# Long convolution with a gate: the last phase's first tiles kept in the filter spectrum's dead tile and loaded from six pairs ahead

## The chip, the core and the metric

The kernel runs on one core of a Trainium2 chip. A core has five engines with instruction streams of their own: TensorE (PE; its weight loads are shown as PEld), VectorE (DVE), ScalarE (ACT), GpSimd (POOL) and SyncE (SP), which only issues transfers. Transfers are moved by 16 DMA engines; here they are issued from SP, ACT and POOL. The metric is the device time of one execution in microseconds (us), as the median of several runs.

## The reference

Two layers, one after the other. The first is a long convolution: `u = x * v` for 4 batches of 12800 positions and 128 channels is convolved along the positions with a filter that a small network makes from a position table, and the result is multiplied by `x`. The second is a gated projection with a convolution of five taps.

```python
h_filt = (np.maximum(pos_emb @ w1, 0.0) @ w2) * window
u = x * v
Uf = np.fft.rfft(u, n=2 * S, axis=1)
Hf = np.fft.rfft(h_filt, n=2 * S, axis=0)
y = np.fft.irfft(Uf * Hf[None], n=2 * S, axis=1)[:, :S]
z = x * y
gate = sigmoid(sum(conv_w[k] * shifted(z, K - 1 - k) for k in range(5)))
out = (gate * (z @ w_val)) @ w_out
```

## The kernel before

Everything is float32. The sequence of 12800 is seen as 2 halves (`J`) of 100 x 64 (`N1`, `N2`), and the convolution is done by transforms of these lengths, as matrix products. There are three phases.

*Phase 1* makes the product of x and v, transforms it along N1 and stores it in DRAM as `a_u`; beside it the filter is transformed into `ag`, a tile of 128 x 12800 floats (51,200 bytes on each partition), the filter's spectrum.

*Phase 2* runs over 50 pairs `p` of rows of the spectrum (`NP = 50`). For a pair, SP loads `a_u` four pairs ahead (L201) and now and then a table of weights (L194); TensorE transforms (L486) and makes the pair's filter from columns 256p to 256p + 255 of `ag` (L467); VectorE multiplies (L492); GpSimd adds (L568, L571); TensorE transforms back. The first half of the result goes through `c_sb` (ScalarE, L508) to the DRAM tile `c_y`, issued from ScalarE (L509). The second half goes through `c_raw` (ScalarE, L530), two pair-steps later GpSimd makes sum and difference of it in `c_both` (L537, two buffers), and it is stored in the DRAM tile `c_z` (L538), from ScalarE for pairs up to 47 and from GpSimd for 48 and 49. Pair 49's `c_y` is stored in two pieces, one copied by ScalarE and issued there, one copied by VectorE and issued from SP (L511 to L514).

*Phase 3* runs over 32 groups of four rows. Group `s` needs its rows of `c_y` or `c_z`: two tiles (`c` = 0, 1) of 100 rows x 2048, each loaded by `load_part(s, c, i)` in three pieces (`PARTS`): `i = 0` are 64 rows (pairs 0 to 31), `i = 1` are 32 (pairs 32 to 47), `i = 2` are 4 (pairs 48 and 49). It needs 0.8 MB of x too (`load_x`, tile `xr`). For each row TensorE multiplies with `inv` (`sd`, L661), ScalarE copies (L666), TensorE transposes (`tp`, L673), ScalarE copies a part (`dif`, L675), VectorE adds and subtracts (`yr`, two buffers, L683 and L684), and GpSimd multiplies with x (L686) into a tile `tail` (for the first group and the 17th) or `ext` (two buffers, each 4 rows of halo and 16 rows). Ten rows later come the taps on VectorE (L703), the sigmoid on ScalarE, the two projections on TensorE (L715, L725) and the output's store.

The order in each engine's stream is that in which the code emits (the loops of phases 2 and 3 are under `manual_schedule`). Rows of groups lie in six tiles `ld` of 128 x 2048, shared with `a_u` and the weights: `buffer()` gives the one that comes free first, and SP waits for its last reader. In phase 2 pieces of the groups 0 to 2 are loaded by the table `early`; the rest and the first three x tiles are loaded at the start of phase 3, when `ag` has been given back.

A transfer issued from SP or ACT counts one of eight completion counters (DMAHW0 to DMAHW7). The program gives them out in turn, in an order of transfers that is fixed when it is built, over both streams; a transfer is issued when the one that had its counter before has landed. Transfers from GpSimd have counters of their own (DMASW).

Of the kernel before, what the change touches and what calls it, by code (L numbers as in the profile page):

```python
# [117 lines left out]
def tile_longconv_gate(  # L118
# [321 lines left out]
    def load_part(s, c, i):  # L440
        j, g = y_order[s]
        if (s, c) not in rows_in:
            rows_in[s, c] = buffer(NP + 1 + s)
        k0, n, step, p0 = PARTS[i]
        to = rows_in[s, c][p0:p0 + step * (n - 1) + 1:step]
        m, n0 = divmod(g * R, H2)
        if j == 0:
            n0 += m * N2 + c * H2
            nc.sync.dma_start(out=to, in_=c_y[k0:k0 + n, n0:n0 + R].rearrange("k p e -> k (p e)"))
        else:  # L450
            if m:
                n0 = H2 - R - n0
            nc.sync.dma_start(
                out=to.rearrange("k (q f) -> k q f", q=2),
                in_=c_z[k0:k0 + n, m, :, c, n0:n0 + R].rearrange("k q i e -> k q (i e)"))

    with tc.tile_pool(name="p2", bufs=1, reuse_waits="tile") as p2, \
# [38 lines left out]
        def inverse(p, vt):  # L496
# [9 lines left out]
            to = c_y[2 * p:2 * p + 2].rearrange("h p e -> p h e")  # L506
            if p < NP - 1:
                nc.scalar.copy(out=c_sb, in_=c_ps)  # L508
                nc.scalar.dma_start(out=to, in_=c_sb)  # L509
            else:  # L510
                nc.scalar.copy(out=c_sb[:, 0], in_=c_ps[:, 0])  # L511
                nc.scalar.dma_start(out=to[:, 0], in_=c_sb[:, 0])
                nc.vector.tensor_copy(out=c_sb[:, 1], in_=c_ps[:, 1])
                nc.sync.dma_start(out=to[:, 1], in_=c_sb[:, 1])  # L514
# [18 lines left out]
        def butterfly(p):  # L533
            raw = raw_p.pop(p)
            both = p2.tile([128, 2, 2, HB], F32, name="c_both", bufs=2)
            for m, op in enumerate((ALU.add, ALU.subtract)):
                nc.gpsimd.tensor_tensor(both[:, :, m], raw[:, :, 1], raw[:, :, 0], op=op)  # L537
            (nc.scalar if p < NP - 2 else nc.gpsimd).dma_start(  # L538
                out=c_z[2 * p:2 * p + 2].rearrange("h s q c i e -> (q c i) (h s) e"),
                in_=both.rearrange("p h s e -> p (h s) e"))  # L540

        filt_p, z_p, v_p, raw_p = {}, {}, {}, {}
        AHEAD = 4

        early = {NP - 5: [(0, 0, 0)], NP - 4: [(0, 1, 0)], NP - 3: [(1, 0, 0)], NP - 2: [(1, 1, 0)],
                 NP - 1: [(0, 0, 1), (0, 1, 1), (2, 0, 0)]}
        with tc.manual_schedule():
            for p in range(-1, NP + 2):
# [43 lines left out]
                for s, c, i in early.get(p, ()):  # L592
                    load_part(s, c, i)

    ag_pool.__exit__(None, None, None)

    with tc.tile_pool(name="p3", bufs=1, reuse_waits="tile") as p3, \
# [7 lines left out]
        tails, exts, loads3, sds, tps, gate_sg, gate_gt, outs3 = {}, {}, {}, {}, {}, {}, {}, {}  # L611

        def load_x(s):
            j, g = y_order[s]
            xr = p3.tile([D, R * ROW], F32, name="xr", bufs=3)
            nc.sync.dma_start(out=xr, in_=xt[j][:, g * R:(g + 1) * R].rearrange("d n b a -> d (n b a)"))
            loads3[s] = xr
# [212 lines left out]


# [39 lines left out]
```

## Time and profile before

| | |
|---|---|
| median of three runs | 1068.72 us |
| lowest and highest run | 1066.05, 1074.51 us |
| the profiled execution, its own time | 1072.18 us |
| span of its instructions | 1070.4 us |
| busy in the span: PE, DVE, POOL, ACT | 973.9, 972.7, 747.4, 625.9 us |
| mean granted clock of TensorE | 0.977 |
| phase 1, to about 332 us: mean DMA rate | 349 GB/s |
| pair loop, 332 to 680 us: mean DMA rate | 316 GB/s |

The span runs from the first instruction to the last. Busy time is an average over stages with different limits: which engine bounds a stage is seen where it has no gaps. In the rows of the timeline the columns are start in us, length in us, engine (SPq and ACTq are the issues of transfers by SP and ScalarE), line, operation, output and input, their shapes, the count of instructions merged in the row, and in brackets the idle time of the engine before it and what ended that. A merged row stands at the start of its first instruction. In the row of a stretch of time the columns are its bounds, its length, the busy time and count of PE, PEld, DVE, ACT and POOL, the granted clock of TensorE, the busy share of the DMA engines and the rate in GB/s.

### The profile page before, as it was taken

Reading aid. Unit: us, or ns where it says so; the run is one execution under the profiler, and the core shown is the slowest. Engines: PE = TensorE matmul, PEld = TensorE weight load, DVE = VectorE, ACT = ScalarE, POOL = GpSimd, SP = SyncE. Lnnn points to the kernel's source line nnn. Section 1 sums busy time; section 2 is a strip of 40 time slices with the busy share of each in tenths; the row PEclk is TensorE's granted clock in tenths of the full one; section 3 lists DMA queues with packets and bytes.
Section 4 is the critical chain, followed back from the end, with each engine's and each line's share of the span. In section 5 each row is a group of like instructions: output and inputs, shape, how many; then the busy total and the mean of one; then the engine's idle time right before and its main releaser. Section 6 shows DMA issues by size and latency. Waiting matters only on the chain. (4 is left out here: it accounts for less than half of the span.)

```text
span 1070.4 us, 21514 instructions
## 1 busy us (share of the span) xinstructions
PE 973.9 (91%) x8080; PEld 510.3 (48%) x8080; DVE 972.7 (91%) x1061; ACT 625.9 (58%) x1017; POOL 747.4 (70%) x465
## 2 busy tenths in 40 slices
PE   2778799999968999999999999779999999999996
PEld 0344466556624555556545555334444444444442
DVE  8878999699938999989999999379999999999997
ACT  1545587798853444434444434367677777777774
POOL 2223222222225999999999999689999999999990
PEclk9989899999988999999999999899999999999999
DMA  8999899988987999979989997977788888888813
GB/s 279 374 345 388 325 381 370 394 327 329 397 290 268 335 317 334 341 277 339 345 307 334 344 335 266 335 294 267 276 294 309 269 295 305 275 300 286 294 75 123
DMA packets 97152, 330.16 MB, mean 308 GB/s; under 512 B 12691, under 2 KB 37883, under 8 KB 81051
## 3 DMA queue, kind: packets, MB, share of 16 engines
q1 hardware_dynamic: 41848, 196.90, 53.8%
q10 hardware_dynamic: 49522, 111.37, 26.9%
q0 software_dynamic: 5680, 20.53, 5.0%
q8 instruction: 66, 1.08, 0.4%
q14 instruction: 36, 0.29, 0.1%
HBM read 197.67 MB, written 131.07 MB: 307 GB/s over the span
## 5 line engine op out<-in xcount | busy, mean ns | idle before, releaser
L686 POOL TENSOR_TENSOR ext<-yr,xr 128x400 f32<-128x400 f32 x120 | 307.7, 2566 | 27.8 <-DVE yr L684 24.5
L703 DVE SCALAR_TENSOR_TENSOR gt<-ext,cw,gt 128x1600 f32<-128x1600 f32 (+1 forms) x132 | 255.1, 1932 | 0.1
L397 POOL DMA_DIRECT2D a_u<-st x64 | 34.4, 537 | 227.5 <-ACT st L389 223.7
L389 ACT COPY st<-fp 128x1024 f32<-128x1024 f32 x128 | 129.7, 1031 | 86.3 <-PE fp L388 42.4
L537 POOL TENSOR_TENSOR c_both<-c_raw 128x512 f32<-128x512 f32 x100 | 126.6, 1295 | 9.8 <-DMA c_z<-c_both 8.7
L530 ACT COPY c_raw<-c_ps 128x1024 f32<-128x1024 f32 x50 | 50.8, 1016 | 140.2 <-PE c_ps L525 124.6
L661 PE MATMUL sd<-ld,inv 128*64 128x512 f32 x512 | 126.5, 612 | 6.7 <-DMA ld<-c_y 6.4
L492 DVE TENSOR_TENSOR va<-z_ps,h_sb 128x2048 f32<-128x2048 f32 x50 | 114.1, 2283 | 20.2 <-PE z_ps L486 20.1
L568 POOL TENSOR_TENSOR va<-va,vb 128x1024 f32<-128x1024 f32 x49 | 116.9, 2386 | 20.2 <-DVE vb L492 17.9
L486 PE MATMUL z_ps<-ld,ld 64*64 64x512 f32 x800 | 112.2, 613 | 19.0 <-DMA ld<-a_u 8.2
L492 DVE TENSOR_TENSOR vb<-z_ps,h_sb 128x2048 f32<-128x2048 f32 x50 | 114.2, 2285 | 13.8 <-POOL va L571 13.8
L666 ACT COPY sd_sb<-sd 128x512 f32<-128x512 f32 x128 | 75.9, 593 | 73.7 <-PE sd L661 61.9
L725 PE MATMUL o_ps<-gd,wout 128*128 128x400 f32 x256 | 111.4, 517 | 8.3 <-DVE gd L720 6.8
L388 PE MATMUL fp<-ld,fsd 64*128 64x512 f32 x320 | 88.6, 656 | 30.7 <-ACT st L389 15.6
L715 PE MATMUL v_ps<-ext,wval 128*128 128x400 f32 x252 | 105.3, 500 | 0.0
L571 POOL TENSOR_TENSOR va<-va,vb 128x1024 f32<-128x1024 f32 x42 | 101.2, 2408 | 0.0
L502 PE MATMUL c_ps<-va,ld 64*64 64x512 f32 x800 | 97.3, 600 | 1.4 <-DVE va L568 1.4
L673 PEld LDWEIGHTS tp<-ident,sd_sb 128*128 128x128 f32 x512 | 58.4, 141 | 77.0 <-PE sd L661 49.6
L720 DVE TENSOR_TENSOR gd<-v_ps,sg 128x400 f32<-128x400 f32 x126 | 84.2, 669 | 0.2 <-ACT sg L708 0.2
L673 PE MATMUL tp<-ident,sd_sb 128*128 128x128 f32 x512 | 80.1, 280 | 3.8 <-DVE yr L684 2.7
L508 ACT COPY c_sb<-c_ps 128x1024 f32<-128x1024 f32 x49 | 49.7, 1014 | 55.5 <-PE c_ps L502 55.5
L683 DVE TENSOR_TENSOR yr<-tp,dif 128x204 f32<-128x204 f32 x128 | 58.8, 459 | 23.9 <-ACT dif L675 23.8
(108 smaller groups left out, 1814.5 us busy)
## 6 DMA issues: line engine op xcount, KB each, us to landing
ld<-a_u SPq DMA_DIRECT2D x48, 1024.0 KB
a_u<-st ACTq DMA_DIRECT2D x62, 512.0 KB
xr<-in_xt_dram SPq DMA_DIRECT2D x32, 800.0 KB
c_y<-c_sb ACTq DMA_DIRECT2D x49, 512.0 KB
out_dram<-o_sb ACTq DMA_DIRECT2D x31, 800.0 KB
c_z<-c_both ACTq DMA_DIRECT2D x48, 512.0 KB
ld<-in_xv_dram SPq DMA_DIRECT2D x40, 512.0 KB
a_u<-st POOLq DMA_DIRECT2D x64, 256.0 KB, 6.3
```

The lines of the kernel that those rows point to most:

```text
L389: nc.scalar.copy(out=st[:, c], in_=fp.rearrange("k j e -> k (j e)"))
L486: nc.tensor.matmul(out=z[half[h], c], lhsT=wk[half[c], 0, half[h]], rhs=a2[half[c], h, j], start=True, stop=True)
L492: nc.vector.tensor_tensor(out, z.rearrange("p (b d) -> p b d", d=D).unsqueeze(1).to_broadcast([128, n, B, D]), h_sb.unsqueeze(2).to_broadc ...
L537: nc.gpsimd.tensor_tensor(both[:, :, m], raw[:, :, 1], raw[:, :, 0], op=op)
L568: (nc.gpsimd if nxt else nc.vector).tensor_tensor(va[:, 0:2], va[:, 0:2], vb[:, 0:2], op=ALU.add)
L571: nc.gpsimd.tensor_tensor(va[:, 2:4], va[:, 2:4], vb[:, 2:4], op=ALU.add)
L661: nc.tensor.matmul(out=to, lhsT=inv[:, 2 if j * m * c else c], rhs=t, start=True, stop=True)
L673: nc.tensor.transpose(out=tp[:, b], in_=t[:, b], identity=ident)
L686: nc.gpsimd.tensor_tensor(e[:, r0 + r], yr, xr, op=ALU.mult)
L703: nc.vector.scalar_tensor_tensor(gt, rows(t, k)[:, cols], cw[:, k:k + 1], gt, op0=ALU.mult, op1=ALU.add)
L715: nc.tensor.matmul(out=v_ps, lhsT=wval, rhs=rows(t)[:, r * ROW:(r + 1) * ROW], start=True, stop=True)
L725: nc.tensor.matmul(out=o_ps, lhsT=wout, rhs=gd, start=True, stop=True)
```

## The change

The first three x tiles, the rows of the second group (`s == 1`) and one of the two `ext` buffers get fixed places in `ag`, whose columns of low number have been read by then: x at columns 0 to 4799 (1600 for each of three), the two row tiles at 4800 and 6848, and the `ext` buffer over the same columns from 4800 to 12799. `ag` lives to the end, and the `p3` pool holds neither `xr` nor that `ext`. The x tiles of all later groups use the three places in turn. The table `early` starts one pair sooner and holds more; pair 49's `c_y` is stored in one piece; the `c_z` stores are taken out of `butterfly` into `store`, and pair 46's is issued a pair later, together with pair 47's.

```diff
     ag = ag_pool.__enter__().tile([128, N1, J, FO], F32, name="ag")
+    AG = ag.rearrange("p k j e -> p (k j e)")
+    XW = R * B * N1
...
         if (s, c) not in rows_in:
-            rows_in[s, c] = buffer(NP + 1 + s)
+            at = 3 * XW + c * 2048
+            rows_in[s, c] = AG[:, at:at + 2048] if s == 1 else buffer(NP + 1 + s)
...
+    def load_x(s):
+        j, g = y_order[s]
+        xr = AG[:, s % 3 * XW:(s % 3 + 1) * XW]
+        nc.sync.dma_start(out=xr, in_=xt[j][:, g * R:(g + 1) * R].rearrange("d n b a -> d (n b a)"))
+        loads3[s] = xr
...
             c_sb = p2.tile([128, 2, BD], F32, name="c_sb", bufs=3)
-            to = c_y[2 * p:2 * p + 2].rearrange("h p e -> p h e")
-            if p < NP - 1:
-                nc.scalar.copy(out=c_sb, in_=c_ps)
-                nc.scalar.dma_start(out=to, in_=c_sb)
-            else:
-                nc.scalar.copy(out=c_sb[:, 0], in_=c_ps[:, 0])
-                nc.scalar.dma_start(out=to[:, 0], in_=c_sb[:, 0])
-                nc.vector.tensor_copy(out=c_sb[:, 1], in_=c_ps[:, 1])
-                nc.sync.dma_start(out=to[:, 1], in_=c_sb[:, 1])
+            nc.scalar.copy(out=c_sb, in_=c_ps)
+            nc.scalar.dma_start(out=c_y[2 * p:2 * p + 2].rearrange("h p e -> p h e"), in_=c_sb)
...
                 nc.gpsimd.tensor_tensor(both[:, :, m], raw[:, :, 1], raw[:, :, 0], op=op)
+            both_p[p] = both
+
+        def store(p):
             (nc.scalar if p < NP - 2 else nc.gpsimd).dma_start(
                 out=c_z[2 * p:2 * p + 2].rearrange("h s q c i e -> (q c i) (h s) e"),
-                in_=both.rearrange("p h s e -> p (h s) e"))
+                in_=both_p.pop(p).rearrange("p h s e -> p (h s) e"))
...
-        early = {NP - 5: [(0, 0, 0)], NP - 4: [(0, 1, 0)], NP - 3: [(1, 0, 0)], NP - 2: [(1, 1, 0)],
-                 NP - 1: [(0, 0, 1), (0, 1, 1), (2, 0, 0)]}
+        early = {NP - 6: ["x0"], NP - 5: [(1, 0, 0), "x1"], NP - 4: [(0, 0, 0), (1, 1, 0)], NP - 3: [(0, 1, 0)],
+                 NP - 2: [(2, 0, 0), (0, 0, 1), (0, 1, 1), (1, 0, 1), (1, 1, 1)]}
...
                 if 0 <= p - 2:
                     butterfly(p - 2)
-                for s, c, i in early.get(p, ()):
-                    load_part(s, c, i)
-
-    ag_pool.__exit__(None, None, None)
+                    for q in () if p == NP - 2 else (p - 3, p - 2) if p == NP - 1 else (p - 2,):
+                        store(q)
+                for what in early.get(p, ()):
+                    if what in ("x0", "x1"):
+                        load_x(int(what[1]))
+                    else:
+                        load_part(*what)
...
         def new_ext(j, q):
-            e = p3.tile([D, HALO + EG * R, B, N1], F32, name="ext", bufs=2)
-            exts[j, q] = e
+            if not ext_buf:
+                ext_buf.append(AG[:, 3 * XW:].rearrange("d (n b a) -> d n b a", b=B, a=N1))
+                ext_buf.append(p3.tile([D, HALO + EG * R, B, N1], F32, name="ext"))
+            exts[j, q] = ext_buf[len(exts) % 2]
...
         with tc.manual_schedule():
-            load_x(0)
-            for c, i in ((0, 2), (1, 2)):
-                load_part(0, c, i)
-            for c, i in ((0, 1), (1, 1), (0, 2), (1, 2)):
-                load_part(1, c, i)
-            load_x(1)
+            for s in range(2):
+                for c in range(2):
+                    load_part(s, c, 2)
             for c, i in ((0, 1), (0, 2), (1, 0), (1, 1), (1, 2)):
                 load_part(2, c, i)
             load_x(2)
...
+    ag_pool.__exit__(None, None, None)
```

ScalarE at the seam, before: from pair 48's `c_y` store to the first copy of phase 3. The names are those of the tiles, with the program's numbers; the three `c_z` sources in this part are pair 46 (`c_both_6161`), pair 47 (`c_both_6217`), and the `c_raw` tiles are pair 48's (`6215`) and pair 49's (`6249`). In brackets stand the counters that an instruction waits for.

```order
L509 DMA c_y_61<-c_sb_6158 128x2x512 [waits DMAHW1_49,Activation_49]
L538 DMA c_z_62<-c_both_6161 128x4x256 [waits DMAHW2_49,Pool_49]
L511 COPY c_sb_6185<-c_ps_6176 128x512 [waits DMAHW3_49,PE_49]
L512 DMA c_y_61<-c_sb_6185 128x512 [waits Activation_49]
L530 COPY c_raw_6215<-c_ps_6190 128x1024 [waits PE_49]
L538 DMA c_z_62<-c_both_6217 128x4x256 [waits DMAHW0_49,Pool_49]
L530 COPY c_raw_6249<-c_ps_6224 128x1024 [waits PE_49]
L666 COPY sd_sb_6295<-sd_6289 128x512 [waits PE_49]
```

The same place in the change (`c_both_6164` is pair 46, `c_both_6221` pair 47, `c_raw_6219` and `c_raw_6251` are pairs 48 and 49):

```order
L518 DMA c_y_61<-c_sb_6161 128x2x512 [waits DMAHW0_49,Activation_49]
L517 COPY c_sb_6191<-c_ps_6182 128x1024 [waits DMAHW7_49,PE_49]
L518 DMA c_y_61<-c_sb_6191 128x2x512 [waits DMAHW1_49,Activation_49]
L534 COPY c_raw_6219<-c_ps_6194 128x1024 [waits PE_49]
L545 DMA c_z_62<-c_both_6164 128x4x256 [waits DMAHW7_49,Pool_49]
L545 DMA c_z_62<-c_both_6221 128x4x256 [waits DMAHW0_49,Pool_49]
L534 COPY c_raw_6251<-c_ps_6226 128x1024 [waits PE_49]
L667 COPY sd_sb_6289<-sd_6283 128x512 [waits DVE_49,PE_49]
```

Both `c_z` stores now stand together behind pair 49's `c_y` store and pair 48's `c_raw`, ahead of pair 49's `c_raw` and of phase 3's copies; before, pair 46's stood ahead of pair 49's `c_y`.

SP at the seam, before: from the last issue that waits for a buffer of the pairs to the second x tile (a piece of 64, 32 or 4 rows is told by its shape; `ld3`, `ld0` are group 0, `ld1`, `ld5` group 1, `ld2` group 2).

```order
L514 DMA c_y_61<-c_sb_6185 128x512 [waits DMAHW4_49,DVE_49]
L449 DMA ld3_78<-c_y_61 32x2048 [waits DMAHW5_49,DMAHW6_49,DMAHW3_49,DMAHW1_49]
L449 DMA ld0_75<-c_y_61 32x2048
L449 DMA ld2_77<-c_y_61 64x2048 [waits DMAHW7_49]
L616 DMA xr_6271<-in_xt_dram 128x1600 [waits DMAHW1_49,Activation_49]
L449 DMA ld3_78<-c_y_61 4x2048 [waits DMAHW4_49,DMAHW3_49,DMAHW2_49]
L449 DMA ld0_75<-c_y_61 4x2048
L449 DMA ld1_76<-c_y_61 32x2048
L449 DMA ld5_80<-c_y_61 32x2048 [waits DMAHW5_49]
L449 DMA ld1_76<-c_y_61 4x2048 [waits DMAHW6_49]
L449 DMA ld5_80<-c_y_61 4x2048 [waits DMAHW7_49]
L616 DMA xr_6279<-in_xt_dram 128x1600 [waits DMAHW0_49]
```

The same place in the change, from the first piece that waits for pair 49's store (`ld3`, `ld0` are group 0, `ag` is group 1 and x, `ld1`, `ld5` group 2):

```order
L452 DMA ld3_78<-c_y_61 4x2048 [waits DMAHW1_49,DMAHW0_49]
L452 DMA ld0_75<-c_y_61 4x2048 [waits DMAHW3_49]
L452 DMA ag_96<-c_y_61 4x2048 [waits DMAHW4_49]
L452 DMA ag_96<-c_y_61 4x2048 [waits DMAHW5_49]
L452 DMA ld1_76<-c_y_61 32x2048 [waits DMAHW6_49]
L452 DMA ld1_76<-c_y_61 4x2048 [waits DMAHW7_49]
L452 DMA ld5_80<-c_y_61 64x2048 [waits PE_49]
L452 DMA ld5_80<-c_y_61 32x2048
L452 DMA ld5_80<-c_y_61 4x2048 [waits DMAHW2_49]
L465 DMA ag_96<-in_xt_dram 128x1600 [waits DMAHW3_49]
```

Of the loads ahead of pair 49's store, four 4-row pieces are left; all else went up into the pairs. By the values that the program waits for, the first of these rows waits for pair 49's `c_y` store (DMAHW1). The sixth takes the counter DMAHW7 and the seventh DMAHW0, and the two `c_z` stores in ScalarE's stream wait for these very transfers: pair 46's for the sixth row, pair 47's for the seventh. Before, pair 46's and 47's stores waited for transfers issued pairs earlier.

More of the change, by code (lines that the diff above doesn't have):

```diff
@@ L455, in load_part @@
                 in_=c_z[k0:k0 + n, m, :, c, n0:n0 + R].rearrange("k q i e -> k q (i e)"))
+    loads3 = {}
+    def load_x(s):
[3 more added lines that the diff above has]
+        loads3[s] = xr
     with tc.tile_pool(name="p2", bufs=1, reuse_waits="tile") as p2, \
@@ L537, in butterfly @@
                 nc.gpsimd.tensor_tensor(both[:, :, m], raw[:, :, 1], raw[:, :, 0], op=op)
+            both_p[p] = both
+        def store(p):
             (nc.scalar if p < NP - 2 else nc.gpsimd).dma_start(
                 out=c_z[2 * p:2 * p + 2].rearrange("h s q c i e -> (q c i) (h s) e"),
-                in_=both.rearrange("p h s e -> p (h s) e"))
-        filt_p, z_p, v_p, raw_p = {}, {}, {}, {}
+                in_=both_p.pop(p).rearrange("p h s e -> p (h s) e"))
+        filt_p, z_p, v_p, raw_p, both_p = {}, {}, {}, {}, {}
         AHEAD = 4
-        early = {NP - 5: [(0, 0, 0)], NP - 4: [(0, 1, 0)], NP - 3: [(1, 0, 0)], NP - 2: [(1, 1, 0)],
-                 NP - 1: [(0, 0, 1), (0, 1, 1), (2, 0, 0)]}
+        early = {NP - 6: ["x0"], NP - 5: [(1, 0, 0), "x1"], NP - 4: [(0, 0, 0), (1, 1, 0)], NP - 3: [(0, 1, 0)],
+                 NP - 2: [(2, 0, 0), (0, 0, 1), (0, 1, 1), (1, 0, 1), (1, 1, 1)]}
         with tc.manual_schedule():
@@ L610, in tile_longconv_gate @@
         groups = [(j, g) for j in range(J) for g in range(NG)]
[L611 to L617, printed above, removed]
+        ext_buf = []
+        tails, exts, sds, tps, gate_sg, gate_gt, outs3 = {}, {}, {}, {}, {}, {}, {}
         def load_rows(s, parts):
```

## The prediction

> **What bounds the kernel now.** I read the 40 slices first, then the chain that ended last, then a table of stages, and last the timeline at the seam between the second and the third phase.
>
> ```profile
> span 1070.4 us, 21514 instructions
> ...
> DVE  8878999699938999989999999379999999999997
> ...
> 332.00:680.00 348.00, 338.44 (x4856) 180.19 (x4848) 329.10 (x198) 149.97 (x244) 331.66 (x188) 0.99 0.90 316
> 680.00:718.00 38.00, 27.06 (x125) 11.52 (x126) 17.96 (x33) 20.68 (x38) 25.14 (x17) 0.91 0.89 340
> 718.00:1028.00 310.00, 309.23 (x1314) 143.29 (x1314) 310.00 (x440) 224.93 (x392) 285.97 (x111) 1.00 0.81 281
> ```
>
> The columns of the stage rows are length, busy PE, PEld, DVE, ACT, POOL, granted clock, DMA share, GB/s. From 718 on VectorE is busy 310.00 of 310.00 us: work shifted there is gained or lost whole at the end. The pair loop (332 to 680) has no large hole. The hole is the seam, where the third phase waits for its first rows. The change touches only this.
>
> ```profile
> 671.45 1.01 ACT L508 COPY c_sb<-c_ps 128x1024 f32<-128x1024 f32 x1 [1.56 <-PE c_ps L502]
> 672.49 0.37 ACTq L509 DMA_DIRECT2D c_y<-c_sb  x1
> ...
> 674.80 0.59 ACT L511 COPY c_sb<-c_ps 128x512 f32<-128x512 f32 x1 [2.33 <-PE c_ps L502]
> ...
> 676.14 0.35 SPq L514 DMA_DIRECT2D c_y<-c_sb  x1
> ...
> 677.45 0.37 ACTq L538 DMA_DIRECT2D c_z<-c_both  x1
> ...
> 678.63 2.49 POOL L537 TENSOR_TENSOR c_both<-c_raw 128x512 f32<-128x512 f32 x2 [1.30 <-DMA c_z<-c_both]
> ...
> 679.28 0.64 PE L525 MATMUL c_ps<-vd,ld 64*64 64x256 f32 x8
> 679.88 0.52 SPq L449 DMA_DIRECT2D ld<-c_y  x1
> 680.46 0.49 SPq L449 DMA_DIRECT2D ld<-c_y  x1
> 681.00 0.47 SPq L449 DMA_DIRECT2D ld<-c_y  x1
> ...
> 681.43 0.82 POOL L538 DMA_DIRECT2D c_z<-c_both  x1 [0.30 <-POOL c_both L537]
> 682.99 2.47 POOL L537 TENSOR_TENSOR c_both<-c_raw 128x512 f32<-128x512 f32 x2 [0.75 <-DMA c_z<-c_both]
> 685.76 0.80 POOL L538 DMA_DIRECT2D c_z<-c_both  x1 [0.30 <-POOL c_both L537]
> 686.32 4.22 PE L661 MATMUL sd<-ld,inv 128*64 128x512 f32 x8 [6.40 <-DMA ld<-c_y]
> 688.87 0.59 ACT L666 COPY sd_sb<-sd 128x512 f32<-128x512 f32 x1 [7.88 <-PE sd L661]
> 690.47 0.76 PE L673 MATMUL tp<-ident,sd_sb 128*128 128x128 f32 x4
> 691.16 1.94 PE L661 MATMUL sd<-ld,inv 128*64 128x512 f32 x8
> ...
> 691.63 0.37 DVE L683 TENSOR_TENSOR yr<-tp,dif 128x204 f32<-128x204 f32 x1 [15.52 <-ACT dif L675]
> 691.91 0.35 DVE L684 TENSOR_TENSOR yr<-tp,dif 128x196 f32<-128x196 f32 x1
> 692.41 1.03 POOL L686 TENSOR_TENSOR tail<-yr,xr 128x400 f32<-128x400 f32 x1 [5.86 <-DMA ld<-c_y]
> 694.05 1.94 PE L661 MATMUL sd<-ld,inv 128*64 128x512 f32 x8
> ...
> 695.91 1.09 PE L673 MATMUL tp<-ident,sd_sb 128*128 128x128 f32 x8
> ...
> 705.10 1.88 DVE L703 SCALAR_TENSOR_TENSOR gt<-ext,cw,gt 128x1600 f32<-128x1600 f32 x1
> ```
>
> TensorE ends the pairs at 679.92 and stands 6.40 us until 686.32, for the last four rows of group 0: their loads are issued from 679.88 on, behind 0.25, 0.25 and 0.5 MB of other rows and an x tile. GpSimd's first product of the third phase comes at 692.41. Between these two moments lies what the change can win.
>
> **The change part by part.**
>
> *Loads moved ahead* (two x tiles, the second group's rows, all 32-row pieces). They leave the seam and run inside pairs 44 to 48. SP issues each where its buffer comes free; none is followed by a load that a pair needs soon. The DMA has room there (rows 634 and 642 below: shares 0.60 and 0.29, beside a full one at 636). I cost this at nothing; the cover is that room, and the price without it stands under the rivals.
>
> ```profile
> 634.00:636.00 2.00, 1.82 (x16) 0.44 (x15) 0.71 (x1) 0.89 (x4) 2.00 (x2) 1.00 0.60 138
> 636.00:638.00 2.00, 0.37 (x4) 0.21 (x8) 2.00 (x2) 0.89 (x1) 1.99 (x3) 1.00 1.01 416
> 642.00:644.00 2.00, 2.00 (x24) 0.60 (x16) 2.00 (x2) 1.43 (x4) 2.00 (x3) 1.00 0.29 30
> 682.00:684.00 2.00, 0.00 (x0) 0.00 (x0) 0.00 (x0) 0.00 (x0) 1.25 (x2) 0.97 1.01 422
> 684.00:686.00 2.00, 0.00 (x0) 0.00 (x0) 0.00 (x0) 0.00 (x0) 1.70 (x3) 0.50 1.05 326
> 690.00:692.00 2.00, 2.00 (x9) 0.86 (x10) 0.37 (x2) 0.92 (x2) 0.00 (x0) 0.82 1.03 423
> ...
> 616.60 0.43 ACTq L538 DMA_DIRECT2D c_z<-c_both  x1
> ...
> 628.06 2.54 POOL L537 TENSOR_TENSOR c_both<-c_raw 128x512 f32<-128x512 f32 x2 [1.76 <-DMA c_z<-c_both]
> ...
> 635.28 2.29 DVE L492 TENSOR_TENSOR vb<-z_ps,h_sb 128x2048 f32<-128x2048 f32 x1 [2.21 <-POOL va L571]
> ...
> 1066.77 0.34 ACTq L738 DMA_DIRECT2D out_dram<-o_sb  x1
> ```
>
> *Pair 49's c_y store in one piece.* ScalarE copies all of it, 1.04 us from copy to issue (671.45 to 672.49), so from 674.80 the store leaves at 675.84, against 676.14 for the second half before. How long a transfer takes with free DMA engines is not shown alone. The last output store (0.41 MB) is issued at 1066.77 and the span ends at 1070.4: at most 3.63 us; 0.41 MB at the 422 GB/s of row 682 is 0.97, which leaves 2.66 as the fixed part. So 0.52 MB takes 3.90 and lands at 679.74. (Before, both halves had landed by 679.88, as the loads behind them show.)
>
> *First rows.* SP's issues stand 0.56 us apart (679.88, 680.46, 681.00). From 679.80 the second 4-row load leaves at 680.36 and, at 2.74, lands at 683.10. TensorE starts then and not at 686.32: 3.2 us won, and with a stand of 3.2 us the clock stays up, so the first eight matmuls take 1.94 and not 4.22: 2.3 more. This is the gain, 5.5 us, if nothing else stands in the way.
>
> *What stands in the way.* The stores of c_z for pairs 46 and 47 now come in ScalarE's stream behind pair 49's work, and they take completion counters that SP's loads had just before: pair 46's waits for the sixth load after pair 49's store, pair 47's for the seventh (front part, the order of ScalarE and SP). ScalarE is a stream in order: behind these two waits stand the last copy of the pairs and every copy of the third phase. The sixth load leaves at 679.80 + 5 x 0.56 = 682.60 and lands at 685.34; the seventh (0.52 MB) leaves at 683.16 and lands at 687.06. So ScalarE issues the stores at 685.4 and 687.1 (pair 47's left at 677.45 before), makes the pairs' last copy (1.01) from 687.5 and reaches the third phase's first copy at 688.5: no more than 0.4 ahead of 688.87. TensorE's transposes then start at 689.2, 1.3 ahead of 690.47, since its sums are done.
>
> *GpSimd.* Its sums of pairs 48 and 49 reuse the buffers that these two stores read, so they wait for the landings. For a c_z store beside loads there are two rows: issued 677.45, waited for until 682.99, 5.54 us; and issued 616.60, waited for until 628.06 (there are two buffers, so sums wait for the store two pairs back), 11.46 us. From below it is 3.90, as above, and I know no reason for less. I take 5.54, since there too SP had just put rows and an x tile into the queues; 3.90 and 11.46 are the ends. Pair 46's store lands at 690.94. Pair 48's sums and store take 681.43 + 0.82 - 678.63 = 3.62, to 694.6; pair 47's store has landed at 692.6; pair 49's take 685.76 + 0.80 - 682.99 = 3.57, to 698.2. GpSimd's first product comes at 698.3 and not 692.41: 5.9 late.
>
> *What this costs.* Two yr tiles exist: VectorE's third row waits for the first product, and TensorE's fifth transposes (second half of row 695.91, so 696.45) wait for that. First product 1.03, step 0.2, yr 0.63 (691.63 to 692.26), step 0.1: 700.26 against 696.45, **3.8 us late**. From there the fill runs as before, TensorE's 2.9 us for two rows (691.16 to 694.05), so nothing is caught up; tap by tap it goes into the stage where VectorE has no gap.
>
> *The rest:* the third phase reads x and one ext buffer from the dead spectrum tile, with the same instructions and shapes: nothing. Added waits of GpSimd on TensorE and ScalarE concern readers two ext tiles back: nothing.
>
> *Sum:* -3.2 - 2.3 (won on TensorE, then waited away) and +3.8 net at the fifth row. The profiled run took 1072.18 us (span 1070.4), 3.46 over the median of 1068.72; on its own time this is 1076.0, on the median **1072.5**.
>
> *Two rules, weighed.* The clock: TensorE stood from 679.92, fell in the window 682 to 684 (0.97, so at 683.9) and was back at 690.7 (0.82). In the change it stands 4.2 us before the first transposes and 5.1 before the fifth. The first drop would be hidden by GpSimd; the second costs one group of sums, 4.22 - 1.94 = 2.3. That is a rival below. The Trainium skill, "TensorE: Matmul & The Clock Gate", section "What's actually happening", says that the half rate comes after an idle window of some 3.4 us that runs freely; an estimate from it is that a stand of 5.1 us holds a whole window about half the time. The trace's single stand agrees. The store: the skill's "DMA: Bandwidth & Descriptors", section "Queues, rings and completion order", says that each DMA engine goes round its queues packet by packet. By it ScalarE's queue with its smaller packets would get a third of the rate beside SP's, and an estimate of the landing is 6.5 us and of the sum 1073.5. The 5.54 of the trace decides; it lies near.
>
> **The rivals.**
> 1. *GpSimd keeps up (faster).* If a lone transfer's fixed part is half of 2.66, the two stores leave near 682.7 and 684.4, the first lands at 685.2 and GpSimd's product comes at 692.6; the fifth transposes at 694.6, 1.9 early: 1066.8. It decides where the first product comes before 694.5, so pair 46's store lands by 687. For it: 2.66 is an upper bound. Against: no c_z row is under 5.5.
> 2. *The clock falls before the fifth transposes:* 3.8 + 2.3, 1074.8. For it: 5.1 us of stand; against: the free phase.
> 3. *The stores land as late as 11.46:* GpSimd 5.9 us later still, 1078.4. For it: up to 3 MB of loads follow pair 49's store; against: the closer row.
> 4. *The loads collide with the pairs:* a stop of the kind at 628.06, which VectorE paid with 2.21: 1074.7. Against: a_u's loads end here.
>
> **How the numbers follow.** The forecast 0.42, rival 1 0.17, rival 2 0.20, rival 3 0.12, rival 4 0.09. The forecast's own range is 1069 to 1076, by 3.90 for the landing and the runs' scatter (1066.05 to 1074.51). Eight in ten: from 1065 (rival 1 with scatter) to 1078. One per cent, 10.7 us, is about what a measurement tells from no change; only the edge of rival 3 and scatter reach it: faster 0.02, same 0.93, slower 0.05.
>
> **What would show it.** In the changed profile: TensorE's first sums near 683 with a clock of 1.00; ScalarE's two c_z issues near 685 and 687, right behind a wait; GpSimd's pairs' sums near 691 and 695 with an idle ended by c_z; the first product near 698; the first tap 3 to 5 us after 705.10. If the first product comes before 694.5, or ScalarE issues both stores before 682, the forecast is wrong and it is faster; if SP's loads stretch the pair loop beyond 680, rival 4 holds.

## The result, and the profile after

The change made the kernel slower by 13 to 15 us, not by the 3.8 of the forecast.

| | kernel before | changed kernel |
|---|---|---|
| median of six runs (lowest to highest) | 1069.2 us (1066.05 to 1420.0) | 1084.32 us (1079.92 to 1091.81) |
| ratio of changed to before, 95% interval | | 1.0139 (1.0104 to 1.0175) |
| the same, measured once more beside other runs | 1071.14 us | 1084.07 us, 1.0130 (1.0096 to 1.0164) |
| profiled execution, its own time and span | 1072.18, 1070.4 us | 1080.71, 1078.9 us |

One run of the kernel before, 1420.0 us, lies far above all others and does not count in the ratio; without it the highest is 1074.51 us.

The timeline of the changed kernel at the seam shows where it went. Columns are as in the prediction; L541 makes the pair sums, L545 stores them, L662, L674, L684, L687 and L704 are the sums, transposes, additions, products and taps of the third phase.

```profile
672.83 0.37 ACTq L518 DMA_DIRECT2D c_y<-c_sb  x1
...
675.64 1.07 SPq L452 DMA_DIRECT2D ld<-c_y  x2
...
676.27 0.64 PE L529 MATMUL c_ps<-vd,ld 64*64 64x256 f32 x8
...
678.10 2.48 PE L662 MATMUL sd<-ld,inv 128*64 128x512 f32 x8 [1.19 <-issue]
...
681.21 3.22 ACTq L545 DMA_DIRECT2D c_z<-c_both  x2
684.48 1.01 ACT L534 COPY c_raw<-c_ps 128x1024 f32<-128x1024 f32 x1 [9.09 <-DMA ld<-c_y]
...
686.03 1.12 PE L674 MATMUL tp<-ident,sd_sb 128*128 128x128 f32 x4 [5.45 <-ACT sd_sb L667]
...
693.35 2.48 POOL L541 TENSOR_TENSOR c_both<-c_raw 128x512 f32<-128x512 f32 x2 [19.02 <-DMA c_z<-c_both]
...
700.57 3.98 POOL L687 TENSOR_TENSOR tail<-yr,ag 128x400 f32<-128x400 f32 x4
701.64 0.37 DVE L684 TENSOR_TENSOR yr<-tp,dif 128x204 f32<-128x204 f32 x1 [9.73 <-POOL tail L687]
...
702.42 1.09 PE L674 MATMUL tp<-ident,sd_sb 128*128 128x128 f32 x4 [8.66 <-DVE yr L685]
...
703.44 3.56 PE L662 MATMUL sd<-ag,inv 128*64 128x512 f32 x8
...
713.23 1.88 DVE L704 SCALAR_TENSOR_TENSOR gt<-ag,cw,gt 128x1600 f32<-128x1600 f32 x1
```

TensorE ends the pairs at 676.91 and has its first rows after 1.19 us, as the change meant. Then everything waits in a row: ScalarE issues two stores (681.21) only when SP's sixth and seventh load have landed, GpSimd waits 19.02 us for the first of them to land, VectorE 9.73 for GpSimd, TensorE 8.66 for VectorE. The first tap comes 36.32 us after TensorE's last pair (713.23 - 676.91); before it was 25.18 (705.10 - 679.92). From the first tap on both kernels run alike: 365.7 and 365.3 us to the end of the span. So the seam alone cost 11.1 us. A second profile of the changed kernel has its first tap 36.07 us after TensorE's last pair, so this stretch repeats within 0.3 us.

Stages of 0.5 us of the changed kernel (columns as in the prediction; the third from the end is the granted clock) show that the clock fell twice, to 0.50 at 682.9 and at 696.5, and came back to 1.00 at 689.7 and at 706.75; before, it fell once:

```profile
682.50:683.00 0.50, 0.00 (x0) 0.00 (x0) 0.00 (x0) 0.00 (x0) 0.00 (x0) 0.86 0.82 301
...
689.50:690.00 0.50, 0.50 (x4) 0.00 (x0) 0.00 (x0) 0.18 (x1) 0.00 (x0) 0.81 0.99 408
...
696.50:697.00 0.50, 0.00 (x0) 0.00 (x0) 0.00 (x0) 0.00 (x0) 0.48 (x2) 0.51 0.00 0
...
706.50:707.00 0.50, 0.50 (x3) 0.07 (x2) 0.00 (x0) 0.00 (x0) 0.00 (x0) 0.75 0.97 358
```

The last pairs lost time too. In the changed kernel:

```profile
639.91 1.01 ACT L517 COPY c_sb<-c_ps 128x1024 f32<-128x1024 f32 x1 [1.11 <-PE c_ps L513]
...
641.42 0.82 ACTq L545 DMA_DIRECT2D c_z<-c_both  x1
...
654.07 2.52 POOL L541 TENSOR_TENSOR c_both<-c_raw 128x512 f32<-128x512 f32 x2 [1.97 <-DMA c_z<-c_both]
...
658.98 1.95 PE L513 MATMUL c_ps<-va,ld 64*64 64x512 f32 x16 [1.04 <-POOL va L575]
```

and the row of the kernel before that answers to the first:

```profile
644.55 1.02 ACT L508 COPY c_sb<-c_ps 128x1024 f32<-128x1024 f32 x1 [1.11 <-PE c_ps L502]
```

From this copy (pair 44's) to TensorE's last pair it is 35.37 us before (679.92 - 644.55) and 37.00 in the changed kernel (676.91 - 639.91). Pair 42's store, issued at 641.42 beside an x tile, rows and a_u, lands some 12 us later; GpSimd, which needs its buffer for pair 44, waits 1.97, and TensorE behind it 1.04. A second profile of the changed kernel gave 40.41, with 3.73 at that wait. Up to pair 44 the changed kernel was 4.64 us ahead here (639.91 against 644.55); over all profiles of this study that row lies between 638.20 and 645.62, so I take this as scatter; whether the change moves the mean of it was not measured. Seam, pairs and scatter make 11.14 + 1.63 - 4.64 and 0.37 at the end: the 8.5 us between the two spans. Without the scatter it is 13, and 16 in the second profile (10.89 at the seam, 5.04 in the pairs); the medians differ by 12.9 and 15.1, which bears this out.

### The profile page after: what moved, and what is told of

The parts are those of the page before. It is cut to its first block, busy times and chain, and to the rows that moved or that the text cites. A ratio compares the mean times of both kernels' runs of the same rounds, so it can differ in the third digit from the quotient of the medians.

```text
span 1078.9 us, 21594 instructions
## 1 busy us (share of the span) xinstructions
PE 975.3 (90%) x8080; PEld 507.3 (47%) x8080; DVE 971.3 (90%) x1060; ACT 626.1 (58%) x1017; POOL 740.7 (69%) x465
## 5 line engine op out<-in xcount | busy, mean ns | idle before, releaser
L687 POOL TENSOR_TENSOR ag<-yr,ag 128x400 f32<-128x400 f32 x64 | 158.3, 2475 | 21.6 <-DVE yr L685 10.7
L687 POOL TENSOR_TENSOR ext<-yr,ag 128x400 f32<-128x400 f32 x56 | 143.2, 2557 | 14.8 <-DVE yr L685 9.0
L541 POOL TENSOR_TENSOR c_both<-c_raw 128x512 f32<-128x512 f32 x100 | 126.6, 1297 | 26.9 <-DMA c_z<-c_both 23.2
L662 PE MATMUL sd<-ld,inv 128*64 128x512 f32 x496 | 122.1, 610 | 1.4 <-issue 1.2
L704 DVE SCALAR_TENSOR_TENSOR gt<-ext,cw,gt 128x1600 f32<-128x1600 f32 (+1 forms) x68 | 120.5, 1772 | 0.1
L704 DVE SCALAR_TENSOR_TENSOR gt<-ag,cw,gt 128x1600 f32<-128x1600 f32 x64 | 120.3, 1879 | 0.0
L674 PEld LDWEIGHTS tp<-ident,sd_sb 128*128 128x128 f32 x512 | 58.9, 142 | 91.6 <-PE sd L662 48.8
L674 PE MATMUL tp<-ident,sd_sb 128*128 128x128 f32 x512 | 81.1, 282 | 17.9 <-DVE yr L685 11.3
L684 DVE TENSOR_TENSOR yr<-tp,dif 128x204 f32<-128x204 f32 x128 | 44.8, 350 | 36.3 <-ACT dif L676 26.2
```

What stands on the lines that cost most here:

```text
L662: nc.tensor.matmul(out=to, lhsT=inv[:, 2 if j * m * c else c], rhs=t, start=True, stop=True)
L674: nc.tensor.transpose(out=tp[:, b], in_=t[:, b], identity=ident)
L687: nc.gpsimd.tensor_tensor(e[:, r0 + r], yr, xr, op=ALU.mult)
L704: nc.vector.scalar_tensor_tensor(gt, rows(t, k)[:, cols], cw[:, k:k + 1], gt, op0=ALU.mult, op1=ALU.add)
```

## The experiments

The theory after this reading (A): GpSimd's waits for the landings of two c_z stores make most of the loss, and ScalarE's wait for SP's loads the rest of it. The rivals: ScalarE alone (B), the loads moved ahead (C), or the putting off of one store. In the table, "pairs" runs from pair 44's copy of c_sb to TensorE's last pair, "42 to 49" between the copies of these pairs (the expectations use it, but it holds a stop between pairs 43 and 44, of 2.0 us in the kernel before and of up to 4.6 in the others), "product" and "tap" are the first of the third phase, after TensorE's last pair. Each from one profile.

| kernel | median, us | ratio to before (95%) | 42 to 49 | pairs | product | tap |
|---|---|---|---|---|---|---|
| before | 1068.7 to 1071.1 | | 45.53 | 35.37 | 12.49 | 25.18 |
| changed | 1084.32 | 1.0139 (1.0104 to 1.0175) | 47.33 | 37.00 | 23.66 | 36.32 |
| c1_again (changed, once more) | 1084.07 | 1.0130 (1.0096 to 1.0164) | 47.78 | 40.41 | 23.27 | 36.07 |
| e1_at_once | 1086.30 | 1.0146 (1.0118 to 1.0173) | 48.58 | 39.29 | 19.84 | 32.61 |
| e2_defer | 1072.20 | 1.0008 (0.9987 to 1.0029) | 43.82 | 35.38 | 14.06 | 26.14 |
| e3_both_ag | 1076.10 | 1.0053 (1.0030 to 1.0076) | 50.55 | 37.18 | 13.30 | 27.26 |
| e4_pool | 1067.77 | 0.9981 (0.9961 to 1.0001) | 47.44 | 38.47 | 8.88 | 21.62 |
| e7_small | 1074.19 | 1.0034 (1.0017 to 1.0052) | 49.56 | 37.37 | 14.44 | 26.65 |
| e9_spread | 1087.24 | 1.0162 (1.0134 to 1.0190) | 50.51 | 42.07 | 22.88 | 35.91 |
| e8_pool_spread | 1070.08 | 0.9992 (0.9971 to 1.0014) | 49.51 | 41.42 | 7.83 | 20.58 |
| e10_pool_xlate | 1070.18 | 1.0014 (0.9993 to 1.0036) | 44.39 | 35.47 | 15.45 | 28.65 |
| e11_pool_end_xlate | 1069.61 | 1.0012 (0.9995 to 1.0029) | 45.73 | 36.20 | 11.20 | 23.95 |
| e12_pool_end | 1064.84 | 0.9955 (0.9937 to 0.9973) | 48.66 | 39.26 | 6.73 | 17.60 |
| e13_x1late | 1061.07 | 0.9929 (0.9907 to 0.9952) | 45.68 | 36.76 | 6.73 | 18.11 |

### GpSimd's wait taken away (e3_both_ag)

```diff
-            both = p2.tile([128, 2, 2, HB], F32, name="c_both", bufs=2)
+            if p < NP - 2:
+                both = p2.tile([128, 2, 2, HB], F32, name="c_both", bufs=2)
+            else:
+                at = 3 * XW + 4096 + (p - NP + 2) * 4 * HB
+                both = AG[:, at:at + 4 * HB].rearrange("p (h s e) -> p h s e", h=2, s=2)
```

> The changed kernel, except that the pair sums of pairs 48 and 49 are written into unused columns of the dead spectrum tile and not into the two c_both buffers. GpSimd then no longer waits for the landing of the c_z stores of pairs 46 and 47; ScalarE still waits for SP's sixth and seventh load before it issues them. Theory A (GpSimd's wait for two landings makes the loss): the sums of pair 48 start some 16 us sooner, the first product comes about 12 us after TensorE's last pair (23.7 in the changed kernel, 12.5 before), the first tap about 24 us after it (36.3 and 25.2), and the time is 1067 to 1073 us. Theory B (what costs is ScalarE, whose copies stand behind the two stores): the first tap stays more than 32 us behind TensorE's last pair and the time above 1079. Theory C (the loads moved ahead cost it, in the pair loop or in the queues): above 1079 too, with an early first product.

Its timeline (line numbers are four higher than in the changed kernel):

```profile
687.19 4.16 ACTq L549 DMA_DIRECT2D c_z<-c_both  x2
691.40 1.01 ACT L534 COPY c_raw<-c_ps 128x1024 f32<-128x1024 f32 x1 [10.12 <-DMA ld<-c_y]
...
692.95 1.11 PE L678 MATMUL tp<-ident,sd_sb 128*128 128x128 f32 x4 [6.17 <-ACT sd_sb L671]
...
696.10 1.04 POOL L691 TENSOR_TENSOR tail<-yr,ag 128x400 f32<-128x400 f32 x1
```

The first product comes 13.30 us after TensorE's end and not 23.66, the first tap 27.26 and not 36.32. GpSimd's wait was worth 9.1 us of the seam; B and C, which asked for 1079 or more, fall as the main cause. The median of 1076.1 is 3 us above the range given: ScalarE's two stores still hold the third phase's copies until 692.3, and the first transposes come 10.2 us after TensorE's end (692.95 - 682.80), no sooner than in the kernel before (10.55).

### ScalarE's wait taken away (e4_pool)

```diff
-            (nc.scalar if p < NP - 2 else nc.gpsimd).dma_start(
+            (nc.scalar if p < NP - 4 else nc.gpsimd).dma_start(
```

> The changed kernel, except that the c_z stores of pairs 46 and 47 are issued from GpSimd, at the same place of the program. They use GpSimd's counters, so ScalarE waits for no load of SP and the stores leave some 6 us sooner; GpSimd still waits for their landings before the sums of pairs 48 and 49. Theory A: pair 46's store leaves about 2 us before TensorE's last pair ends and not 4.3 after; with a landing of 5.5 to 12 us the first product comes 11 to 17.5 us after TensorE's end (23.7 in the changed kernel) and the time is 1067 to 1076 us. Theory B: ScalarE is free, the time is at or below 1069 whatever GpSimd waits for. Theory C: above 1079.

```profile
677.11 1.59 POOL L545 DMA_DIRECT2D c_z<-c_both  x2
...
681.26 2.48 POOL L541 TENSOR_TENSOR c_both<-c_raw 128x512 f32<-128x512 f32 x2 [2.57 <-DMA c_z<-c_both]
...
686.86 0.66 PE L674 MATMUL tp<-ident,sd_sb 128*128 128x128 f32 x4
...
688.64 1.02 POOL L687 TENSOR_TENSOR tail<-yr,ag 128x400 f32<-128x400 f32 x1 [0.26 <-DVE yr L685]
```

Pair 46's store now leaves at 677.11, ahead of SP's loads (from 679.92 in this run), and has landed by 681.26, 4.15 us later. One edit frees ScalarE and makes the landing early, and the whole loss of the seam is gone: the tap at 21.62, 14.7 us sooner than in the changed kernel and 3.6 sooner than before. Of the 14.7, the 9.1 of e3 belong to GpSimd's wait; 5.6 are left for ScalarE's, by this difference only, since no run frees ScalarE alone. A and B both expected this time, so it was e3 that told them apart.

### The store at once, and the putting off alone (e1_at_once, e2_defer)

e1 puts pair 46's store back to its old place in the changed kernel; e2 is the kernel before with `butterfly` and `store` apart as in the change, and nothing else.

```diff
-                    for q in () if p == NP - 2 else (p - 3, p - 2) if p == NP - 1 else (p - 2,):
-                        store(q)
+                    store(p - 2)
```

> The changed kernel with pair 46's c_z store issued at once, as before, and all else as changed. Pair 47's store still takes the counter that SP's sixth load after pair 49's c_y store had. Theory A: the sums of pair 48 run at once, those of pair 49 still wait for pair 47's store, which leaves some 4 us after TensorE's end and lands some 12 later; the first product comes 3.6 us sooner than in the changed kernel, about 20 us after TensorE's end, and the time is 1076 to 1081 us: putting the store off is a small part of the loss. Rival (putting the store off is the whole loss): at or below 1070.

> The kernel before with one part of the change alone: pair 46's c_z store is put off by a pair and issued together with pair 47's. Here both take counters that earlier transfers had, so ScalarE waits for no load of the third phase. Theory A: pair 46's store leaves some 2 us before TensorE's end; with a landing of 5.5 to 12 us the sums of pair 48 begin 3 to 9 us after TensorE's end, the first product 10.5 to 16.5 us after it (12.5 before), and the time is 1067 to 1074 us, so the part alone costs little. Rival (putting the store off is the whole loss): 1080 or more.

The timeline of e1, then that of e2:

```profile
686.57 0.38 ACTq L545 DMA_DIRECT2D c_z<-c_both  x1
...
699.27 2.47 POOL L541 TENSOR_TENSOR c_both<-c_raw 128x512 f32<-128x512 f32 x2 [14.04 <-DMA c_z<-c_both]
```

```profile
676.17 1.08 ACTq L541 DMA_DIRECT2D c_z<-c_both  x2
...
685.46 2.49 POOL L537 TENSOR_TENSOR c_both<-c_raw 128x512 f32<-128x512 f32 x2 [9.40 <-DMA c_z<-c_both]
```

In e1 the wait has only moved to pair 47's store (issued 686.57, landed 699.27, 12.7 us); the product came at 19.84, as expected. The time did not: 1086.3, above the 1076 to 1081 given. Its profile shows pairs of 39.29 and an up-to-pair-44 of 643.73, some 4 to 5 us more than the two profiles of the changed kernel (639.91 and 638.82); how much of that is scatter and how much the store's place stays open. That putting the store off is the whole loss is refuted, by e1 and by e2, where that part alone cost nothing that can be measured (1.0008): there pair 46's store leaves at 676.17 and lands in 9.3 us, and TensorE has its first rows only at 685.98 anyway.

### Why the landing takes 12 us (e7_small)

e7 leaves out seven eighths of the bytes of some loads behind pair 49's store, so that its third and fourth group are computed from other data.

```diff
-        if j == 0:
+        if s in (2, 3) and (s, c, i) != (2, 0, 0):
+            n0 += m * N2 + c * H2
+            nc.sync.dma_start(out=to[:, 0:256], in_=c_y[k0:k0 + n, n0:n0 + R].rearrange("k p e -> k (p e)")[:, 0:256])
+        elif j == 0:
...
+        w = 200 if s == 2 else XW
```

> The changed kernel with an eighth of the bytes in the loads of the third and fourth group's rows (but for the 64 rows that are loaded in the pairs) and of the third x tile; the rest of those tiles holds what lay there before, so the third and fourth group are computed from other data. Number and order of all instructions are as in the changed kernel. Crowd theory (a c_z store lands late because SP's megabytes go through the same DMA engines): pair 46's store lands 4 to 6 us after its issue and not 12; ScalarE issues it some 1 us sooner too; the first product comes 14 to 17 us after TensorE's end (23.7 in the changed kernel) and the time is 1071 to 1077 us. Rival (a store of such small packets takes 12 us whatever runs beside it, or its wait is for something else): it lands some 12 us after its issue and the time is 1081 or more.

```profile
683.17 1.64 ACTq L549 DMA_DIRECT2D c_z<-c_both  x2
...
686.82 2.49 POOL L545 TENSOR_TENSOR c_both<-c_raw 128x512 f32<-128x512 f32 x2 [9.76 <-DMA c_z<-c_both]
```

With an eighth of the bytes beside it the store lands in 3.65 us, with the same instructions in the same order on each engine. So it is the bytes. How they hold it up is in the DMA view of the changed kernel, for 681 to 684, 684 to 687 and 687 to 690 us (queue 1 is SP's, queue 10 ScalarE's; packets, MB, share of the 16 engines' time):

```profile
q1 hardware_dynamic: 153, 0.91, 92.4%
```

```profile
q1 hardware_dynamic: 140, 0.87, 87.0%
q10 hardware_dynamic: 47, 0.05, 4.5%
```

```profile
q1 hardware_dynamic: 157, 0.96, 76.6%
q10 hardware_dynamic: 275, 0.28, 26.3%
```

The store was issued at 681.21, but until 687 ScalarE's queue moved 0.05 MB and SP's 1.78. As many bytes as it has are through only near 691 (0.33 MB by 690, and 0.37 more between 690 and 692), and GpSimd goes on at 693.35, when nearly all of both stores are (1.01 MB by 693.4); the view does not tell the packets of the two apart. In e7 the same queue moved 0.51 MB between 684 and 686, beside no fewer packets of SP's, but small ones (158 packets, 0.11 MB).

Two delays add up here. ScalarE's first packets move some 4 us after the issue (between 685.0 and 685.5), and 0.9 us after it in e7 and for pair 49's c_y store in the changed kernel. Then the queues take turns by packets, and SP's are the larger ones, 6.0 KB against 1.0. This is seen best in e1, for 692 to 696 us:

```profile
q1 hardware_dynamic: 241, 1.45, 87.4%
q10 hardware_dynamic: 239, 0.24, 17.2%
```

So while SP's queue has work, ScalarE's store gets about a seventh of the bytes.

### The last pairs (c1_again, e9_spread, e8_pool_spread, e10_pool_xlate)

c1 is the changed kernel itself. e9 moves the x tiles from pairs 44 and 45 to 46 and 47; e8 is e9 with e4's stores; e10 has e4's stores and both x tiles in pair 48, behind the rows.

```diff
-        early = {NP - 6: ["x0"], NP - 5: [(1, 0, 0), "x1"], NP - 4: [(0, 0, 0), (1, 1, 0)], NP - 3: [(0, 1, 0)],
+        early = {NP - 5: [(1, 0, 0)], NP - 4: [(0, 0, 0), (1, 1, 0), "x0"], NP - 3: [(0, 1, 0), "x1"],
```

> The changed kernel itself once more, beside the same runs of the kernel before. If the two losses add (about 11 us at the seam between the phases and 2 to 3 in the last pairs), it is 12 to 15 us over the kernel before: 1082 to 1086 us. In the profile the first tap comes 35 to 37 us after TensorE's last pair, and the time from pair 42's to pair 49's copy of c_sb is 47 to 49 us (45.5 in the profile of before).

> The changed kernel with the first two x tiles loaded two pairs later (pairs 46 and 47 and not 44 and 45), where no a_u is loaded any more. Collision theory (the x tiles in pairs 44 and 45, beside a_u, make c_z stores land late, so that GpSimd's sums of pair 45 and with them pair 47 wait): the time from pair 42's to pair 49's copy of c_sb falls by 1.5 to 3 us, back to 45 to 46, and the whole by as much, to 1080 to 1083 us; the seam stays at 35 to 37. Rival (the pairs' stop is not the x tiles'): no change from the changed kernel, 1083 to 1086.

> Both edits together: the c_z stores of pairs 46 and 47 issued from GpSimd, and the first two x tiles loaded two pairs later. If the seam and the pairs are separate losses, the seam is 21 to 22.5 us (25.2 before), the pairs take 45 to 46 from pair 42 to 49, and the time is 1064 to 1067 us, under the kernel before by 3 to 6. If the x tiles now crowd pair 46's and 47's stores instead, GpSimd waits for these and the time is 1068 or more.

> The c_z stores of pairs 46 and 47 from GpSimd, and the first two x tiles loaded in pair 48, behind the rows there: from 660 to 680 us the DMA engines were busy only 0.4 to 0.8 of the time, while from 636 to 660 they were full. Collision theory in its second form (the pairs' stop depends on bytes in the full stretch, wherever in pairs 44 to 47 the x tiles stand): the time from pair 42's to pair 49's copy of c_sb is 44 to 46.5 us (47.4 with the x tiles in pairs 44 and 45 and the same stores), the seam 21 to 23, the time 1062 to 1067. Rival (the rows moved ahead, not the x tiles, stop the pairs; or the x tiles now crowd pair 49's c_y store): 1068 or more, with the pairs at 47 or more or the seam above 24.

The timeline of e9:

```profile
641.92 0.43 ACTq L545 DMA_DIRECT2D c_z<-c_both  x1
...
655.35 2.51 POOL L541 TENSOR_TENSOR c_both<-c_raw 128x512 f32<-128x512 f32 x2 [2.74 <-DMA c_z<-c_both]
...
661.65 2.51 POOL L541 TENSOR_TENSOR c_both<-c_raw 128x512 f32<-128x512 f32 x2 [1.48 <-DMA c_z<-c_both]
...
672.55 3.69 PE L513 MATMUL c_ps<-va,ld 64*64 64x512 f32 x16 [3.49 <-DVE va L575]
```

The expectation of e9 and e8 fell: two pairs later the x tiles cost more (42.07 and 41.42); in e9 GpSimd waited for two late c_z stores and not for one. So the collision theory as first put, that it is a_u beside them, is wrong. In pair 48 (e10) the stop is gone: 35.47 against 35.37 before. So the x tiles' bytes in the stretch where the engines are full make the stop, and the rows moved ahead do not. All profiles agree: "pairs" is 37.00 to 40.41 in the seven with both x tiles in pairs 44 and 45, 41.42 and 42.07 with them in 46 and 47, 36.76 with one alone in 44 (e13), 35.47 and 36.20 with both in 48, and 35.37 and 35.38 with none. But e10 is no faster, because the bytes are then in front of pair 49's c_y store:

```profile
664.54 1.06 SPq L465 DMA_DIRECT2D ag<-in_xt_dram  x2
...
669.59 0.37 ACTq L518 DMA_DIRECT2D c_y<-c_sb  x1
...
673.03 0.64 PE L529 MATMUL c_ps<-vd,ld 64*64 64x256 f32 x8
...
680.11 1.06 SPq L452 DMA_DIRECT2D ld<-c_y  x2
...
682.94 4.01 PE L662 MATMUL sd<-ld,inv 128*64 128x512 f32 x8 [9.27 <-DMA ld<-c_y]
```

The store issued at 669.59 releases SP's 4-row loads at 680.11, 10.5 us later, and TensorE stands 9.27 us. In the changed kernel it took 2.81 (672.83 to 675.64).

### Versions that beat both (e12_pool_end, e11_pool_end_xlate, e13_x1late)

All three have the edits of e3 and e4, and issue the last four c_z stores behind the last sums. e11 loads both x tiles in pair 48; e13 keeps the first in pair 44 and loads the second at the seam, behind the four loads of 4 rows.

```diff
-                    for q in () if p == NP - 2 else (p - 3, p - 2) if p == NP - 1 else (p - 2,):
+                    for q in () if NP - 2 <= p <= NP else range(NP - 4, NP) if p > NP else (p - 2,):
                         store(q)
```

> The changed kernel, except that the sums of pairs 48 and 49 go into unused columns of the dead spectrum tile, and the c_z stores of pairs 46 to 49 are all issued from GpSimd behind these sums. Nobody waits for the landing of a c_z store at the seam and ScalarE for no load, and no c_z store runs beside pair 49's c_y store. Theory: TensorE's first sums start 1 to 2.5 us after its last pair, the clock holds through them, the first product comes 7 to 9 us after TensorE's end, and the first tap 18 to 20.5 us (21.6 with the stores of pairs 46 and 47 issued ahead of the sums); the time 1064 to 1069 us. Rival (the four issues on GpSimd, some 3.2 us, make the first product late, or the crowd of loads makes the rows late): the first tap 22 us or more after TensorE's end.

> The same with the first two x tiles loaded in pair 48. If the gains add: the pairs at 44 to 46.5 us from pair 42 to 49, the first tap 18 to 20.5 us after TensorE's last pair, the time 1060 to 1065 us, faster than the kernel before by 6 to 10. If the x tiles crowd pair 49's rows, the first tap comes 22 us or more after TensorE's end and the time is 1066 or more.

> The version with all four last c_z stores on GpSimd behind the sums, the first x tile in pair 44 as in the changed kernel, and the second x tile loaded at the seam, behind the four loads of 4 rows (the second group needs it some 16 us after TensorE's last pair). If the pairs' stop goes with the bytes, 0.8 MB less in the full stretch halves it: 46 to 47.5 us from pair 42's to pair 49's copy of c_sb (48.7 in the same version with both x tiles in the pairs), with the seam still at 17.5 to 19, and the time 1061 to 1064 us. If 0.8 MB at the seam makes the third group's rows late instead, the seam is 20 or more and the time 1065 or more.

The timeline of e13:

```profile
675.27 0.64 PE L529 MATMUL c_ps<-vd,ld 64*64 64x256 f32 x8
...
676.73 0.44 SPq L465 DMA_DIRECT2D ag<-in_xt_dram  x1
...
677.08 2.49 PE L666 MATMUL sd<-ld,inv 128*64 128x512 f32 x8 [1.17 <-issue]
...
682.64 3.13 POOL L691 TENSOR_TENSOR tail<-yr,ag 128x400 f32<-128x400 f32 x3
...
694.02 1.88 DVE L708 SCALAR_TENSOR_TENSOR gt<-ag,cw,gt 128x1600 f32<-128x1600 f32 x1
```

e12 came at 1064.84 and e13 at 1061.07, both times inside what was expected; e13 is 0.7% (0.5 to 0.9) faster than the kernel before. TensorE stands 1.17 us, the clock stays at 1.00 over the whole seam, the product comes at 6.73 and the tap at 18.11, and the pairs take 36.76 and not the 39.26 of e12 (two profiles of one kernel can differ as much, see the changed kernel's 37.00 and 40.41). e11 missed its range (1069.61): with both x tiles in pair 48, pair 49's c_y store was again late, though less than in e10, where c_z stores ran beside it (7.0 us from its issue to SP's 4-row loads, against 10.5).

## Why the prediction was wrong

The direction and the chain were right, the size was not: 3.8 us were forecast, 12.9 to 15.1 came. Step by step:

- *First rows*: right. TensorE started after 1.19 us (3.2 forecast), since pair 49's store took 2.81 us and not 3.90, and the second 4-row load 1.9 (issued at 676.21) and not 2.74.
- *What stands in the way*: right. The two issues on ScalarE were put at 5.5 and 7.2 us after TensorE's last pair; they came at 4.3 and about 7.2. The first transposes were put at 9.3 and came at 9.1.
- *GpSimd*: this is the term that was mis-sized. "I take 5.54, since there too SP had just put rows and an x tile into the queues." Pair 46's store took 12.1 us (681.21 to 693.35), and 12.8 in the second profile. In the row of 5.54 the store left 2.4 us before the long run of SP's loads (679.88); here it left in the middle of it. e4 (ahead of the loads, 4.15), e7 (an eighth of the bytes, 3.65) and the DMA view (1.78 MB of SP's first) show it. The prediction had 11.46 as the upper end, close to what came; the choice should have been made by the bytes queued at that moment, and not by the nearest row. SP had issued 2.6 MB of loads from 675.64 on, of which the DMA view shows 0.57 MB moved by 681.21: some 2 MB stood in its queue (an estimate from these rows).
- *What this costs*: the sums and stores after the landing took 7.2 us (7.4 forecast), so the product was 11.2 us later than before. The slack at the fifth row was 2.2 (700.57 to 702.42 is 1.85, before 4.04), as forecast 2.1; and the clock, which fell at 696.5, took 2.2 back: from the fifth row's transposes to the first tap 10.81 us against 8.65.
- *Loads moved ahead*, costed at nothing: wrong by 1.6 and 5.0 us in two profiles. The cover named (DMA room in rows 634 and 642) was used up by what was moved there: from 640 to 660 us the DMA share is 0.75 in the kernel before and 1.03 in the changed one. Rival 4 had the place and the wait right and put it at 2.2.
- *The chances*: rivals 2, 3 and 4 came all at once. They were counted as alternatives with 0.20, 0.12 and 0.09, but rival 3 brings rival 2 with it: a store that lands late makes TensorE stand longer (8.66 us), and a longer stand loses the clock. 3.8 + 5.9 + 2.3 + 2.2, all from the prediction, make 14.2, between the 12.9 and the 15.1 that were measured. The upper end of the range held only one of them.

On the rules that were weighed: the clock fell 2.3 us after TensorE's first sums had ended (680.58) and 2.7 us into the stand of 8.66 us, sooner than in the one stand that the prediction had (4.0 us). The Trainium skill, "TensorE: Matmul & The Clock Gate", section "What's actually happening", puts the half rate behind an idle window of some 3.4 us that runs freely. The trace agrees with the window but not with its being idle: TensorE was busy in 0.33 and 0.20 of the 3.41 us ahead of the two falls.

The estimate of 6.5 us for the landing came from the Trainium skill, "DMA: Bandwidth & Descriptors", section "Queues, rings and completion order", by which each DMA engine goes round its queues packet by packet. The trace agrees with the turns once ScalarE's packets move (241 and 239 in e1). What the estimate had wrong is the share, a third: with a seventh of 422 GB/s and the 2.66 us of the prediction it gives 11.3 us, and with the 4 us until the first packet in place of the 2.66 it gives 12.7 (estimates); 12.1 was measured. What held ScalarE's first packets back for 4 us is not shown by any run here.

## What to carry to other kernels

A transfer's landing time is not a property of the transfer: count the bytes that stand in the queues when it is issued, on the other queues too, and compare the sizes of the packets that take turns. One engine's wait for a transfer's counter and another's for the same transfer's landing add up, so before loads are moved ahead, look which stores then come behind them and who needs their buffers. Rivals that feed each other belong in the range together, not side by side.

## What was not expected of the hardware

A store of 0.52 MB was waited for 2.8 us after its issue (c_y in the changed kernel, in packets of 2 KB), 3.65 (e7, c_z from ScalarE, packets of 1 KB), 4.15 (e4, c_z from GpSimd, on a queue of its own with packets of about 4 KB), 9.3 (e2), 10.5 (c_y in e10) and 12.1 to 12.8 us (changed, e1).

The clock fell after shorter stands than the 4.0 us seen before. In e1 TensorE's rows and the stage of 2 us around them are:

```profile
683.74 2.37 PE L661 MATMUL sd<-ld,inv 128*64 128x512 f32 x8 [0.72 <-DMA ld<-c_y]
688.54 0.89 PE L673 MATMUL tp<-ident,sd_sb 128*128 128x128 f32 x4 [2.43 <-ACT sd_sb L666]
```

```profile
688.00:690.00 2.00, 1.46 (x6) 0.79 (x8) 0.17 (x1) 1.31 (x3) 0.00 (x0) 0.70 0.94 375
```

It stood 2.43 us, was at work again, and the clock fell at 688.8 (a mean of 0.70 over the two us is 0.8 us at full rate and 1.2 at half). In e13 a stand of 1.17 us cost nothing.

What decides is in the times of the changes. In the changed kernel they are 682.86, 689.69, 696.51 and 706.75 us: 2, 2 and 3 times 3.41 us apart. From 630 to 725 us the profiles of this study have 30 falls and 30 returns, and in each profile all of them lie whole multiples of 3.41 us apart. Cut each profile into these stretches of 3.41 us: the clock fell at the end of every one in which TensorE was busy for 0.43 of the time or less, and held behind every one with 0.48 or more; from half it came back behind stretches with 0.88 or more and not with 0.74 or less (busy time by the modelled ends of the matmuls). In e1 the stretch up to the fall was busy for 0.29. So a stand shorter than a stretch can cost the clock, if it fills more than half of one.
